# Derivative in place, two gradients transposed by DMA, and a packed score block in a four-layer transformer's forward and backward pass

## The chip, the cores and the metric

The kernel runs on one core of one Trainium2 chip. The metric is the device time of the whole program in microseconds; the median of 7 runs stands for a kernel.

## The reference

Four residual layers on x of 2048 tokens by 640, in bfloat16, with 32 heads of 20. Layers 0 and 2 (kind A) are linear attention with the features phi; layers 1 and 3 (kind B) are attention in a causal window of 256. All four have a layernorm in front and a projection behind; layers of the same kind share their weights. The outputs are x after four layers, and the gradients of x and of the four weights for a given gradient of the output.

```python
def _A_ref(x, wqkv, wo):                       # H = 32, Dh = 20
    q, k, v = ...                              # x @ wqkv, split in heads
    phi = lambda t: jnp.where(t > 0, t + 1, jnp.exp(t)) + 1e-6
    pq, pk = phi(q), phi(k)
    kv = jnp.einsum("bhsd,bhse->bhde", pk, v)
    z = jnp.einsum("bhsd->bhd", pk)
    num = jnp.einsum("bhqd,bhde->bhqe", pq, kv)
    den = jnp.einsum("bhqd,bhd->bhq", pq, z)[..., None] + 1e-6
    return ... (num / den) ... @ wo

def _B_ref(x, wqkv, wo):                       # W = 256
    scores = jnp.einsum("bhqd,bhkd->bhqk", q, k) * (Dh ** -0.5)
    mask = (idx[:, None] - idx[None, :] >= 0) & (idx[:, None] - idx[None, :] < W)
    p = _softmax(jnp.where(mask[None, None], scores, -1e9), axis=-1)
    return ... jnp.einsum("bhqk,bhkd->bhqd", p, v) ... @ wo

x = x + _A_ref(_layernorm(x), A_wqkv, A_wo);  x = x + _B_ref(_layernorm(x), B_wqkv, B_wo)
x = x + _A_ref(_layernorm(x), A_wqkv, A_wo);  x = x + _B_ref(_layernorm(x), B_wqkv, B_wo)
# outputs: x, and jax.vjp of all this at grad_out: A_x, A_wqkv, A_wo, B_wqkv, B_wo
```

The derivative of phi, where only the stored feature p = phi(t) is at hand, is min(p − 1e-6, 1).

## The kernel before

**Tiles and order.** The 2048 tokens are 16 tiles of 128. The order of the instructions of TensorE (PE), VectorE (DVE), ScalarE (ACT) and GpSimd (POOL) is the program's own: each stage is a plan, a list of pairs of a slot and a function, and a loop runs the functions slot by slot. The slots of the parts stand in tables, `PLACES`. All DMAs are issued on one queue, SyncE's (SP), in the order that a scheduler gives them. Two helpers record most of TensorE's instructions, so many rows of the profile have their lines: L138 is a matmul, L162 and the two copies at L165 and L167 are `flip`, a transpose on TensorE through the identity and its copy out of PSUM. L108 is the DMA.

**Stages.** The forward of layer 0 runs up to some 115 us. The score steps of layer 1 follow up to 400, those of layer 3 from 427 to 686; beside the steps run layernorms, projections and the rest of layer 2's linear attention as filling (`plan_front`; table `f3` has the slots beside layer 3's steps). From 690 to 1165 is the backward of layer 3's attention, from 1165 to 1285 that of layer 2's linear attention, from 1295 to 1740 that of layer 1's. From 1804 to 2031 the linear backward of layer 0 runs with the weight-gradient matmuls (`wg`, accumulated over tokens from `lhs` and `rhs` that DMAs bring from DRAM) as filling: after each slot, `fill(0.8)` gives 8 of them. What is left of the weight gradients runs alone to the end at 2251.

**Score steps.** A step is one token tile t with one group of 4 heads; 8 steps make a tile, 128 steps a layer. The keys of a tile of queries are 3 blocks of 128 tokens (from the third tile on): the far block, whose lower triangle is kept, the middle one, which is whole, and the diagonal one, whose upper triangle is kept. The scores lie with the keys on the partitions. `f_scores` (L370) does 12 matmuls of 32 rows (the padded head) by 128 keys by 128 queries, four heads in four row groups, into `sT`, a PSUM tile of four banks with one buffer; the exponential at L385 reads 4 x 384 columns of it into `eT`. `f_masks` (L388) sets the masked triangles to zero on POOL (L391 the diagonal block, L395 the far one). Two steps later `b_pv` (L213) multiplies the blocks of `eT` with v into `ops`, and `ob` (L231) divides by the sums.

**Linear backward.** `plan_linear` (L927) has the parts of one tile, table `l2`; a tile starts every 8 slots. `load` brings `ldn`, `lv`, `lpqk` (the features of q and k, [128, 2 x 640] a tile), `lhn` and `lg` for two tiles. `turn` transposes three of them. `part` (L949) makes 320 columns of the gradients of q, k or v by matmuls into PSUM; for q and k, `fd` (L969) first works out the derivative of phi for these columns, and L971 multiplies:

```python
nc.vector.scalar_tensor_tensor(out=f, in0=src(...)[:, c * CW:(c + 1) * CW], scalar=-EPS,
                               in1=self.one.to_broadcast([P, CW]), op0=ALU.add, op1=ALU.min)
nc.vector.tensor_tensor(out=dst, in0=ps[:, 0:CW], in1=f, op=ALU.mult)
```

The result `dqa` [128, 1920] holds dq, dk and dv. `dh` (L991) needs it transposed, in `dqT`: the q part by a DMA transpose (`turn_q`; layer 0's first four tiles, and none of layer 2's, by TensorE, `by_pe`), the k and v parts by `turn_kv`, 5 transposes on TensorE (L983) and a copy each, on DVE (L986) for k and on ACT (L988) for v. `dh` multiplies k, v and q in this order with the transposed weights; `ln` and `ln2` (L1004, L1014) do the layernorm's backward, with POOL's additions at L1012 and L1019. Layers 2 and 0 both use this plan.

Of the kernel before, what the change touches and what calls it, by code (L numbers as in the profile page):

```python
# [17 lines left out]
H = 32  # L18
DH = 20
HP = 32  # L20
T = 2048
TT = T // P
DT = D // P
# [17 lines left out]
PLACES = dict(  # L41
    f1=[0.1, 1.7, 2.5, 6.6, 9.6, 12, 13.2, 14.1, 14.5, 14.6, 14.5, 16.1],
    f2=[-27.5, -23.6, -21.5, -20.6, -19.5, -17.9, -16.5, -15.1, -13.5, -7.8, -6.9, -5.5, -4.7, -3.8, -2.9, 11, 12, 13, 14, 17.6, 22.4, 23.3, 24, 25.1, 26.4, 27.3],
    f3=[-35.7, -30, -26.5, -25, -24, -23.8, -22.5, -18, -16.4, -14, -12.1, -7.4, -6.8, -6, -4.9, -3.5, -1.7, 11.3, 12.4, 13.4],
    bf=[2.1, 3.1, 5.2, 14.9, 17.9, 6.2, 7.8, 10, 14.6, 28.3],
    bh=[13.1, 14.5, 15.5, 17.1, 17.5, 18, 20, 21.2, 25.7, 28.3, 30, 36, 19.1, 20.1, 21.8, 22.5, 23.3, 24.6, 25.2, 27.5, 30.5, 31.7, 33, 35, 41.5, 43, 2.2, 8.3, 9.5, 12, 18.9, 34.5],
    l2=[-10.4, -1.3, 0.6, 1.2, 1.9, 3.2, 4.6, 6.2, 7, 7.5, 5, 8, 8.3, 10.2, 11.8, 14, 14.4, 15.4, 16, 16.2, 18.7],
    n1=[9.7, 0.5, 3.3, 3.6, 5.3, 9, 3, 4.7, 5.4, 5.6, 24],
    xx=[1, 1, 0, 0, 0, 0, 1, 1, 0, 0, 0, 0, 0, 1, 0, 0, 1, 0, 0, 0, 0, 0, 0, 1, 0, 0, 1, 0, 0, 0, 1, 0],
    bd=[0, 0, 1, 0, 0, 0, 1, 0, 0, 0, 0, 0, 0, 1, 1, 0, 0, 1, 1, 0, 1, 0, 1, 0, 1, 0, 1, 1, 0, 1, 1, 0])  # L50
# [2 lines left out]
class Kern:  # L53
    def __init__(self, ctx, tc, x0, A_w, A_wo, B_w, B_wo, grad, outs):
        self.ctx, self.tc = ctx, tc
        self.nc = nc = tc.nc
        self.W = dict(A=A_w, B=B_w)
        self.Wo = dict(A=A_wo, B=B_wo)
        self.grad = grad
        self.out_x4, self.out_gx, dWA, dWoA, dWB, dWoB = outs  # L60
        self.dW = dict(A=dWA, B=dWB)
        self.dWo = dict(A=dWoA, B=dWoB)
        self.serial = 0

# [24 lines left out]
        nc.gpsimd.affine_select(out=self.bm, in_=self.bm, compare_op=ALU.is_ge, fill=0.0, base=0,  # L89
                                pattern=[[-DH, HB], [0, HA]], channel_multiplier=1)  # L90
        nc.gpsimd.affine_select(out=self.bm, in_=self.bm, compare_op=ALU.is_ge, fill=0.0, base=DH - 1,
                                pattern=[[DH, HB], [0, HA]], channel_multiplier=-1)
        self.mhalf = const.tile([P, 1], F32, name="mhalf")
        nc.gpsimd.memset(self.mhalf, -0.5)
        self.rs = [const.tile([P, TT], F32, name=f"rs{l}") for l in range(4)]
        self.r = [const.tile([P, TT, H], F32, name=f"r{l}") for l in range(4)]
        self.mz = {l: const.tile([KB, 6, KA], BF, name=f"mz{l}") for l in (0, 2)}
        self.mzT = {l: const.tile([KA, 6, KB], BF, name=f"mzT{l}") for l in (0, 2)}
        self.one = const.tile([P, 1], BF, name="one")
        nc.gpsimd.memset(self.one, 1.0)  # L100
        self.dmz = const.tile([KB, 6, KA], BF, name="dmz")
        self.dmzT = const.tile([KA, 6, KB], BF, name="dmzT")
        self.macc = const.tile([KB, 6, KA], F32, name="macc")
# [109 lines left out]
    def b_pv(self, st, l, t, g, e, nb, rings, o):  # L213
        nc = self.nc
        q = g % 4
        if q == 0:
            st.ops = st.po.tile([P, HALF, HA], F32, name="ops")
            st.first = None
        for hh in range(4):
            for i in range(nb):  # L220
                ins = self.mm(st.ops[:, 4 * q + hh, :], e[:, hh, i * P:(i + 1) * P],
                              rings[i]["s"][:, 2, 4 * g + hh, 0:HA], st.first is None, i == nb - 1)
# [12 lines left out]


    def forward(self, st):
# [11 lines left out]
        st.sm = self.pool(keep, "fm", 4, side="right")  # L249
        st.fa = self.pool(keep, "fa", 3, side="right")  # L250
        st.xm = self.pool(keep, "xm", 5, side="right")
        st.fpe = self.pool(keep, "pe", 5, side="right")
        wo = self.pool(keep, "wo", 1, side="right")
        rings = {i: self.pool(keep if i in (0, 3, 4) else early, f"ring{i}", 1, side="right") for i in (0, 3, 4, 1, 2)}
        st.fb = self.pool(early, "fb", 3, side="right")
# [87 lines left out]
        def run(n):  # L343
            u, fs = None, slots[n]
            if B1 <= n < B1 + G * TT:
                if n == B1:
                    for f in fs:
                        f()
                    fs = []
                u = self.f_scores(st, *divmod(n - B1, G), X[1])  # L350
            elif B3 <= n < END:
                u = self.f_scores(st, *divmod(n - B3, G), X[3])
# [17 lines left out]
    def f_scores(self, st, t, g, X):  # L370
# [8 lines left out]
        for i in range(nb):  # L379
            for hh in range(4):  # L380
                r0 = HP * hh
                self.mm(s[:, hh, i * P:(i + 1) * P], rings[i]["T"][r0:r0 + HP, 1, g, :], qT[r0:r0 + HP, 0, g, :],
                        True, True, (r0, 0))
        e = st.fpe.tile([P, 4, 3 * P], BF, name="eT")
        nc.scalar.activation(e[:, :, 0:nb * P], s[:, :, 0:nb * P], ACT.Exp)  # L385
        return t, g, e, nb, rings, X[t]["ob"]

    def f_masks(self, t, g, e, nb, rings, o):  # L388
        nc = self.nc
        dg = e[:, :, (nb - 1) * P:nb * P]  # L390
        nc.gpsimd.affine_select(out=dg, in_=dg, compare_op=ALU.is_ge, fill=0.0, base=0,  # L391
                                pattern=[[0, 4], [1, P]], channel_multiplier=-1)
        if nb == 3:
            fr = e[:, :, 0:P]
            nc.gpsimd.affine_select(out=fr, in_=fr, compare_op=ALU.is_ge, fill=0.0, base=-1,  # L395
                                    pattern=[[0, 4], [-1, P]], channel_multiplier=1)

    def plan_ln(self, st, l, t, x, src, key, pool):

# [527 lines left out]
    def plan_linear(self, st, lp, l, t, X, WT, g_out):  # L927
# [21 lines left out]
        def part(nm, c):  # L949
# [15 lines left out]
            if nm == "pk":  # L965
                nc.scalar.copy(dst, ps[:, 0:CW])
            else:
                f = lp.le.tile([P, CW], BF, name="fd")
                nc.vector.scalar_tensor_tensor(out=f, in0=src("pq" if nm == "dn" else "pk")[:, c * CW:(c + 1) * CW], scalar=-EPS,  # L969
                                               in1=self.one.to_broadcast([P, CW]), op0=ALU.add, op1=ALU.min)  # L970
                nc.vector.tensor_tensor(out=dst, in0=ps[:, 0:CW], in1=f, op=ALU.mult)  # L971

        def turn_q():
            x["dT"] = st.sp.tile([P, NF, P], BF, name="dqT", bufs=3)
# [3 lines left out]
                self.dma(x["dT"][:, 0:DT, :], x["dqkv"][:, 0:D], transpose=True)  # L978

        def turn_kv(j):  # L980
            ps = st.ps.tile([P, 8, P], BF, name="flip", tag="m")
            for k in range(DT):
                nc.tensor.transpose(ps[:, k, :], x["dqkv"][:, j * D + k * P:j * D + (k + 1) * P], self.ident)  # L983
# [42 lines left out]
        fs += [lambda n=n, ci=ci: dh(n, ci) for ci in range(2) for n in range(3)] + [ln, ln2]  # L1026
# [385 lines left out]
```

The softmax here doesn't subtract the row's maximum and nothing guards it: scores larger than these inputs give would overflow.

## Time and profile before

| | us |
|---|---|
| median of 7 runs | 2252.49 |
| lowest and highest | 2242.76, 2260.34 |
| profiled execution | 2252.86 |
| its span | 2251.1 |
| TensorE busy | 2076.8 |
| DVE busy | 1454.9 |
| ACT busy | 1356.7 |
| POOL busy | 1089.6 |
| mean granted clock of TensorE | 0.978 |
| DMA moved | 449.50 MB, mean 200 GB/s |

One execution is profiled; its time is 1.76 us longer than its span, the first to the last instruction. Rows of groups give the line, the engine, the operation, out<-in, shapes and count, then busy time and mean ns of one, then idle time of the engine ahead of them with what ended it. Rows of a timeline give start and length in us, and in brackets an idle time ahead and what ended it; several matmuls in one row are a run of them, and since matmuls are pipelined, rows overlap: what one holds is read from the start of the next. Rows by stage give start:end, the span, busy time and count of each engine, TensorE's granted clock, the share of the 16 DMA engines in use, and GB/s.

### The profile page before, as it was taken

The page shows a single profiled execution, that of the slowest core. Times are in us where ns is not written, and L with a number is a line of the kernel's source. Part 1 is how long each engine was busy: PE and PEld are TensorE (multiplying, and loading weights), DVE is VectorE, ACT ScalarE, POOL GpSimd, SP SyncE. Part 2 cuts the span into 40 slices and gives each one's busy share as a digit, 9 for nine tenths or more (in the row PEclk, how much of TensorE's full clock was granted, in tenths as well). Part 3 has the DMA queues.
Part 4 walks back from the last instruction along what each step waited for, and adds up shares of the span by engine and source line. Part 5 has one row for each costly group of instructions (what it writes and reads, how often), then busy time and mean ns, then how long its engine had stood idle before and what let it go on. Part 6 is the DMA issues. An engine that isn't in the chain of part 4 may idle for free. (4 is left out here: it accounts for less than half of the span.)

```text
span 2251.1 us, 76829 instructions
## 1 busy us (share of the span) xinstructions
PE 2076.8 (92%) x32061; PEld 1691.9 (75%) x32061; DVE 1454.9 (65%) x2934; ACT 1356.7 (60%) x2109; POOL 1089.6 (48%) x1888
## 2 busy tenths in 40 slices
PE   7889998899989999998979899999988899999999
PEld 5667776577767877777757678777777788889998
DVE  6778885777744788887749858787876245550000
ACT  5467887377776888887746668788876233430000
POOL 2046665156666677777534456777765312220000
PEclk9899999999999999999999989999999999999999
DMA  7489885698879589998799733999987998857753
GB/s 258 140 237 230 225 222 150 166 220 216 206 209 239 150 182 204 209 216 180 160 288 260 200 91 104 194 206 210 203 185 158 270 300 250 255 159 199 201 143 90
DMA packets 721357, 449.50 MB, mean 200 GB/s; under 512 B 461296, under 2 KB 697840, under 8 KB 720624
## 3 DMA queue, kind: packets, MB, share of 16 engines
q1 hardware_dynamic: 721008, 444.58, 77.9%
q8 instruction: 251, 4.11, 0.8%
q14 instruction: 98, 0.80, 0.1%
HBM read 213.09 MB, written 149.82 MB: 161 GB/s over the span
## 5 line engine op out<-in xcount | busy, mean ns | idle before, releaser
L665 DVE TENSOR_TENSOR ds<-dp,e 128x768 bf16<-128x768 f32 (+2 forms) x512 | 464.2, 907 | 174.6 <-PE s L138 62.9
L662 ACT ACTIVATE e<-s 128x768 bf16<-128x768 f32 (+2 forms) x512 | 395.6, 773 | 137.2 <-PE s L138 104.2
L385 ACT ACTIVATE eT<-sT 128x1536 bf16<-128x1536 f32 (+2 forms) x256 | 350.8, 1370 | 132.1 <-PE sT L138 130.2
L138 PE MATMUL wg<-rhs,lhs 128*128 128x240 bf16 (+1 forms) x3840 | 374.1, 256 | 8.8 <-DMA lhs<-o 7.3
L138 PEld LDWEIGHTS <-lhs 128*128 128x128 bf16 x3840 | 337.0, 98 | 23.9 <-DMA lhs<-o 8.3
L674 POOL TENSOR_SCALAR_AFFINE_SELECT e<-e 128x256 bf16<-128x256 bf16 x512 | 207.1, 406 | 252.0 <-ACT e L662 247.2
L138 PEld LDWEIGHTS <-dqT 128*128 128x128 bf16 x1920 | 170.6, 98 | 64.8 <-issue 10.4
L391 POOL TENSOR_SCALAR_AFFINE_SELECT eT<-eT 128x512 bf16<-128x512 bf16 x256 | 162.3, 635 | 109.6 <-ACT eT L385 108.8
L138 PE MATMUL acc<-slabqs,ds 128*128 128x20 bf16 x2880 | 210.4, 172 | 1.4 <-ACT dq L744 0.5
L138 PE MATMUL dp<-slabvT,dT 32*128 32x384 bf16 (+2 forms) x1024 | 168.7, 322 | 45.1 <-DVE ds L665 40.2
L138 PE MATMUL acc<-ds,e 128*128 128x20 bf16 x2880 | 208.3, 172 | 0.0
L138 PEld LDWEIGHTS <-ds 128*128 128x128 bf16 x2880 | 188.1, 96 | 12.0 <-issue 3.5
L678 POOL TENSOR_SCALAR_AFFINE_SELECT e<-e 128x256 bf16<-128x256 bf16 x448 | 195.9, 437 | 0.0
L138 PEld LDWEIGHTS <-e 128*128 128x128 bf16 x2880 | 170.2, 96 | 10.9 <-issue 1.8
L1012 POOL TENSOR_TENSOR dh<-dh,lg 128x640 f32<-128x640 f32 x32 | 51.5, 1609 | 254.1 <-DVE s L1009 244.8
L685 PE MATMUL flip<-ident,ds 128*128 128x128 bf16 x1944 | 170.8, 222 | 3.3 <-DVE ds L772 1.2
L138 PE MATMUL s<-slabkT,slabqT 32*128 32x384 bf16 (+2 forms) x1024 | 168.8, 325 | 4.6 <-ACT dT L797 3.3
L1094 DVE CAST wr<-wg 128x240 bf16<-128x240 f32 (+1 forms) x72 | 27.2, 378 | 222.4 <-PE wg L138 219.4
L1092 ACT CAST wr<-wg 128x240 bf16<-128x240 f32 (+1 forms) x48 | 16.3, 339 | 254.9 <-PE wg L138 227.6
L138 PE MATMUL dense<-WB,hnT 128*128 128x320 bf16 x960 | 165.3, 304 | 3.2 <-DVE o L459 1.8
L138 PE MATMUL dense<-WTA,dqT 128*128 128x320 bf16 x960 | 160.9, 299 | 3.1 <-DMA dqT<-dqa 2.7
L138 PE MATMUL acc<-slabks,dsT 128*128 128x20 bf16 x2880 | 147.4, 172 | 11.9 <-DMA dsT<-ds 11.9
(176 smaller groups left out, 4606.4 us busy)
## 6 DMA issues: line engine op xcount, KB each, us to landing
rhs<-dqkv SPq DMA_DIRECT2D x64, 480.0 KB, 4.9
s<-s SPq DMA_DIRECT2D x32, 768.0 KB, 3.8
T<-T SPq DMA_DIRECT2D x32, 768.0 KB, 3.9
dqkv<-dq SPq DMA_DIRECT2D x16, 960.0 KB, 5.6
dqkv<-dqa SPq DMA_DIRECT2D x32, 480.0 KB, 5.1
slabkT<-T SPq DMA_DIRECT2D x56, 256.0 KB, 4.3
slabvT<-T SPq DMA_DIRECT2D x56, 256.0 KB, 3.6
slabks<-s SPq DMA_DIRECT2D x56, 256.0 KB, 3.7
```

The source lines that it names most:

```text
L138: return self.nc.tensor.matmul(out, lhsT=lhsT, rhs=rhs, start=start, stop=stop, skip_group_check=True, **kw)
L385: nc.scalar.activation(e[:, :, 0:nb * P], s[:, :, 0:nb * P], ACT.Exp)
L391: nc.gpsimd.affine_select(out=dg, in_=dg, compare_op=ALU.is_ge, fill=0.0, base=0, pattern=[[0, 4], [1, P]], channel_multiplier=-1)
L662: nc.scalar.activation(u.e[:, :, 0:u.cw], s[:, :, 0:u.cw], ACT.Exp)
L665: nc.vector.tensor_tensor(out=d.ds[:, :, 0:d.cw], in0=d.dp[:, :, 0:d.cw], in1=d.e[:, :, 0:d.cw], op=ALU.mult)
L674: nc.gpsimd.affine_select(out=dg, in_=dg, compare_op=ALU.is_ge, fill=0.0, base=0, pattern=[[0, 2], [-1, P]], channel_multiplier=1)
L678: nc.gpsimd.affine_select(out=fr, in_=fr, compare_op=ALU.is_ge, fill=0.0, base=-1, pattern=[[0, 2], [1, P]], channel_multiplier=-1)
L685: nc.tensor.transpose(ps[:, 3 * j + i, :], f.ds[:, j, i * P:(i + 1) * P], self.ident)
L1012: nc.gpsimd.tensor_tensor(out=x["dh"], in0=x["dh"], in1=L["g"][:, i, :], op=ALU.add)
L1092: nc.scalar.copy(o[:, 0:w], ps[:, 0:w])
L1094: nc.vector.tensor_copy(o[:, 0:w], ps[:, 0:w])
```

## The change

Three parts.

**Derivative in place** (layers 2 and 0). The derivative of phi is worked out in place, over `lpqk`, for 640 columns at once by one tensor_scalar each for q (slot −2.3, before the `turn` of `ldn`) and k (slot 4.4, after the `turn` that reads the features of k). The four `fd` and the constant tile `one` go; L971's multiplication reads the changed `lpqk`.

```diff
-    l2=[-10.4, -1.3, 0.6, 1.2, ..., 16, 16.2, 18.7],
+    l2=[-10.4, -1.3, 0.6, 1.2, ..., 16, 16.2, 18.7, -2.3, 4.4],
...
-                f = lp.le.tile([P, CW], BF, name="fd")
-                nc.vector.scalar_tensor_tensor(out=f, in0=src("pq" if nm == "dn" else "pk")[:, c * CW:(c + 1) * CW], scalar=-EPS,
-                                               in1=self.one.to_broadcast([P, CW]), op0=ALU.add, op1=ALU.min)
-                nc.vector.tensor_tensor(out=dst, in0=ps[:, 0:CW], in1=f, op=ALU.mult)
+                nc.vector.tensor_tensor(out=dst, in0=ps[:, 0:CW], in1=src("pq" if nm == "dn" else "pk")[:, c * CW:(c + 1) * CW], op=ALU.mult)
+
+        def slope(nm):
+            nc.vector.tensor_scalar(out=src(nm), in0=src(nm), scalar1=-EPS, scalar2=1.0, op0=ALU.add, op1=ALU.min)
```

**Layer 0's k and v gradients by DMA.** From the fifth tile of layer 0 on, `turn_kv` issues a DMA transpose in place of the five transposes on TensorE and the copy; `dh`, `ln` and `ln2` of these tiles run 5 slots later.

```diff
         def turn_kv(j):
+            if lp.by_pe and t >= 4:
+                self.dma(x["dT"][:, j * DT:(j + 1) * DT, :], x["dqkv"][:, j * D:(j + 1) * D], transpose=True)
+                if j == 2:
+                    self.dma(self.rows(self.dq[l], t), x["dqkv"])
+                return
...
+        if lp.by_pe and t >= 4:
+            a = a[:13] + [v + 5 for v in a[13:21]] + a[21:]
```

**Packed scores of layer 3.** Where a step has three blocks, the far one is split by queries. Its first 64 queries go, with all keys, into columns 256 to 319. Of its last 64 queries only keys 64 to 127 can be inside the window, and these 64 x 64 scores are put where the diagonal block is masked anyway: on partitions 64 to 127, columns 128 to 191. So a head has 320 columns, the exponential reads 4 x 320, and 16 matmuls make them: 8 of 128 x 128, 4 of 128 keys by 64 queries, 4 of 64 keys by 64 queries. On POOL a first select copies the 64 x 64 scores to columns 320 to 383 with their mask, the other two mask the diagonal block and the 64 columns of the far one. The lower half of columns 320 to 383 is set to zero once in each of the five `eT` buffers, which are now a fixed list. `b_pv` takes the blocks in the order `(i + 2) % 3`.

```diff
+        if self.halves and nb == 3:
+            for c0, i, q0, n, k0 in ((0, 1, 0, P, 0), (P, 2, 0, P, 0), (2 * P, 0, 0, HALFP, 0), (P, 0, HALFP, HALFP, HALFP)):
+                for hh in range(4):
+                    score(hh, c0, rings[i], q0, n, k0)
+            w = 5 * HALFP
...
+        nc.scalar.activation(e[:, :, 0:w], s[:, :, 0:w], ACT.Exp)
...
+        if self.halves and nb == 3:
+            keep(e[HALFP:P, :, 5 * HALFP:6 * HALFP], e[HALFP:P, :, P:P + HALFP], HALFP, False)
+            dg = e[:, :, P:2 * P]
+            keep(dg, dg, P, True)
+            fr = e[:, :, 2 * P:2 * P + HALFP]
+            keep(fr, fr, HALFP, False)
...
-    f3=[-35.7, -30, -26.5, -25, -24, -23.8, -22.5, -18, -16.4, -14, -12.1, -7.4, -6.8, -6, -4.9, -3.5, -1.7, 11.3, 12.4, 13.4],
+    f3=[-35.7, -29.4, -26.6, -25, -24, -23.8, -22.2, -18, -16.5, -15, -13.1, -7.7, -6.8, -6, -4.4, -3.4, -1.7, 11.3, 12.4, 13.4],
```

More of the change, by code (lines that the diff above doesn't have):

```diff
@@ L20 @@
 HP = 32
+HALFP = P // 2
 T = 2048
@@ L43 @@
     f2=[-27.5, -23.6, -21.5, -20.6, -19.5, -17.9, -16.5, -15.1, -13.5, -7.8, -6.9, -5.5, -4.7, -3.8, -2.9, 11, 12, 13, 14, 17.6, 22.4, 23.3, 24, 25.1, 26.4, 27.3],
-    f3=[-35.7, -30, -26.5, -25, -24, -23.8, -22.5, -18, -16.4, -14, -12.1, -7.4, -6.8, -6, -4.9, -3.5, -1.7, 11.3, 12.4, 13.4],
+    f3=[-35.7, -29.4, -26.6, -25, -24, -23.8, -22.2, -18, -16.5, -15, -13.1, -7.7, -6.8, -6, -4.4, -3.4, -1.7, 11.3, 12.4, 13.4],
     bf=[2.1, 3.1, 5.2, 14.9, 17.9, 6.2, 7.8, 10, 14.6, 28.3],
     bh=[13.1, 14.5, 15.5, 17.1, 17.5, 18, 20, 21.2, 25.7, 28.3, 30, 36, 19.1, 20.1, 21.8, 22.5, 23.3, 24.6, 25.2, 27.5, 30.5, 31.7, 33, 35, 41.5, 43, 2.2, 8.3, 9.5, 12, 18.9, 34.5],
-    l2=[-10.4, -1.3, 0.6, 1.2, 1.9, 3.2, 4.6, 6.2, 7, 7.5, 5, 8, 8.3, 10.2, 11.8, 14, 14.4, 15.4, 16, 16.2, 18.7],
+    l2=[-10.4, -1.3, 0.6, 1.2, 1.9, 3.2, 4.6, 6.2, 7, 7.5, 5, 8, 8.3, 10.2, 11.8, 14, 14.4, 15.4, 16, 16.2, 18.7, -2.3, 4.4],
     n1=[9.7, 0.5, 3.3, 3.6, 5.3, 9, 3, 4.7, 5.4, 5.6, 24],
@@ L98, in __init__ @@
         self.mzT = {l: const.tile([KA, 6, KB], BF, name=f"mzT{l}") for l in (0, 2)}
-        self.one = const.tile([P, 1], BF, name="one")
-        nc.gpsimd.memset(self.one, 1.0)
         self.dmz = const.tile([KB, 6, KA], BF, name="dmz")
@@ L220, in b_pv @@
             for i in range(nb):
-                ins = self.mm(st.ops[:, 4 * q + hh, :], e[:, hh, i * P:(i + 1) * P],
+                b = (i + 2) % 3 if self.halves and nb == 3 else i
+                ins = self.mm(st.ops[:, 4 * q + hh, :], e[:, hh, b * P:(b + 1) * P],
                               rings[i]["s"][:, 2, 4 * g + hh, 0:HA], st.first is None, i == nb - 1)
@@ L251, in forward @@
         st.xm = self.pool(keep, "xm", 5, side="right")
-        st.fpe = self.pool(keep, "pe", 5, side="right")
+        fpe = self.pool(keep, "pe", 1, side="right")
+        st.fe, self.halves = [fpe.tile([P, 4, 3 * P], BF, name=f"eT{i}") for i in range(5)], False
         wo = self.pool(keep, "wo", 1, side="right")
@@ L351, in run @@
             elif B3 <= n < END:
+                if n == B3:
+                    self.halves = True
+                    for e in st.fe:
+                        nc.gpsimd.memset(e[0:HALFP, :, 5 * HALFP:6 * HALFP], 0.0)
                 u = self.f_scores(st, *divmod(n - B3, G), X[3])
@@ L378, in f_scores, with score @@
         s = st.pS.tile([P, 4, 512], F32, name="sT")
[L379 to L385, printed above, removed]
+        e = st.fe[0]
+        st.fe.append(st.fe.pop(0))
+        def score(hh, c0, k, q0, n, k0=0):
+            r0 = HP * hh
+            self.mm(s[k0:P, hh, c0:c0 + n], k["T"][r0:r0 + HP, 1, g, k0:P], qT[r0:r0 + HP, q0:q0 + n], True, True, (r0, k0))
+        qT = qT[:, 0, g, :]
+        if self.halves and nb == 3:
[3 more added lines that the diff above has]
+            w = 5 * HALFP
+        else:
+            for i in range(nb):
+                for hh in range(4):
+                    score(hh, i * P, rings[i], 0, P)
+            w = nb * P
+        nc.scalar.activation(e[:, :, 0:w], s[:, :, 0:w], ACT.Exp)
         return t, g, e, nb, rings, X[t]["ob"]
@@ L389, in f_masks, with keep @@
         nc = self.nc
[L390 to L396, printed above, removed]
+        def keep(out, in_, w, up):
+            s = 1 if up else -1
+            nc.gpsimd.affine_select(out=out, in_=in_, compare_op=ALU.is_ge, fill=0.0, base=0 if up else -1,
+                                    pattern=[[0, 4], [s, w]], channel_multiplier=-s)
+        if self.halves and nb == 3:
[4 more added lines that the diff above has]
+            keep(fr, fr, HALFP, False)
+        else:
+            dg = e[:, :, (nb - 1) * P:nb * P]
+            keep(dg, dg, P, True)
+            if nb == 3:
+                fr = e[:, :, 0:P]
+                keep(fr, fr, P, False)
     def plan_ln(self, st, l, t, x, src, key, pool):
@@ L1025, in plan_linear @@
         fs += [turn_q, lambda: turn_kv(1), lambda: turn_kv(2)]
-        fs += [lambda n=n, ci=ci: dh(n, ci) for ci in range(2) for n in range(3)] + [ln, ln2]
+        fs += [lambda n=n, ci=ci: dh(n, ci) for ci in range(2) for n in range(3)] + [ln, ln2, lambda: slope("pq"), lambda: slope("pk")]
+        if lp.by_pe and t >= 4:
+            a = a[:13] + [v + 5 for v in a[13:21]] + a[21:]
         return ([(a[0], load)] if i == 0 else []) + list(zip(a[1:], fs))
```

## The prediction

> **What bounds the kernel now.** I read the page first, then busy time by stage for the three places where the change acts, then the timelines of the engines that are full there.
>
> ```profile
> span 2251.1 us, 76829 instructions
> ## 1 busy us (share of the span) xinstructions
> PE 2076.8 (92%) x32061; PEld 1691.9 (75%) x32061; DVE 1454.9 (65%) x2934; ACT 1356.7 (60%) x2109; POOL 1089.6 (48%) x1888
> ...
> L385 ACT ACTIVATE eT<-sT 128x1536 bf16<-128x1536 f32 (+2 forms) x256 | 350.8, 1370 | 132.1 <-PE sT L138 130.2
> ```
>
> TensorE is busy for 92%, so on average little else can matter. By stage (start:end, span, then busy time of each engine, clock, DMA share, GB/s) it differs:
>
> ```profile
> 455.88:620.36 164.48, 154.91 (x2795) 119.37 (x2793) 123.84 (x321) 128.42 (x110) 101.52 (x169) 1.00 0.85 216
> 620.36:686.31 65.95, 54.39 (x1041) 42.58 (x1044) 29.75 (x74) 47.13 (x35) 44.38 (x75) 0.95 0.78 217
> 1183.38:1272.18 88.80, 81.66 (x950) 65.47 (x949) 83.03 (x157) 59.83 (x121) 39.99 (x29) 1.00 0.90 240
> 1850.00:1930.00 80.00, 80.00 (x877) 71.34 (x876) 45.30 (x89) 32.99 (x68) 18.60 (x12) 1.00 0.94 269
> 1930.00:2030.00 100.00, 100.00 (x1068) 88.70 (x1067) 51.38 (x100) 38.15 (x80) 24.73 (x16) 1.00 0.65 181
> ```
>
> Rows 1 and 2 are layer 3's forward score steps: TensorE lacks 9.6 and 11.6 us. Row 3 is layer 2's backward: DVE (83.0 of 88.8) is fuller than TensorE (81.7). Rows 4 and 5 are layer 0's backward beside weight gradients: TensorE is full, and DMA too in row 4. The clock is full but for a little in row 2.
>
> In layer 3, TensorE's timeline shows one loop through the exponential:
>
> ```profile
> 588.74 0.45 PE L138 MATMUL ops<-s,eT 128*128 128x21 bf16 x12
> 589.43 0.29 PE L138 MATMUL sT<-T,T 32*128 32x128 bf16 x8 [0.24 <-ACT eT L385]
> 589.54 0.24 PE L138 MATMUL sT<-T 32*128 32x128 bf16 x4
> 589.71 0.85 PE L138 MATMUL dense<-WB,hnT 128*128 128x320 bf16 x5
> 590.40 0.44 PE L162 MATMUL flip<-ident,o 128*128 128x128 bf16 x5
> 590.68 0.45 PE L138 MATMUL ops<-s,eT 128*128 128x21 bf16 x12
> ```
>
> The score tile sT has one buffer: its next 12 matmuls wait until the exponential has read it. A step is 1.98 us: 0.48 from the first score matmul to the exponential's start, 1.45 of exponential (128x1536), 0.05 to restart. TensorE stands 0.19 to 0.28 of each such step. Of the 8 steps of a tile, five are like this, two are bound by TensorE itself (2.03 us) and one waits 0.25 for an `ob` copy (2.44).
>
> Layer 2's DVE runs without a gap; a tile is 7.24 us, and four `fd` rows are in it:
>
> ```profile
> 1232.31 0.48 DVE L969 SCALAR_TENSOR_TENSOR fd<-lpqk,one 128x320 bf16<-128x320 bf16 x1
> 1232.88 0.49 DVE L971 TENSOR_TENSOR dqa<-dense,fd 128x320 bf16<-128x320 f32 x1
> 1233.29 1.11 DVE L969 SCALAR_TENSOR_TENSOR fd<-lpqk,one 128x320 bf16<-128x320 bf16 x1
> 1234.50 0.49 DVE L971 TENSOR_TENSOR dqa<-dense,fd 128x320 bf16<-128x320 f32 x1
> 1234.91 1.31 DVE L969 SCALAR_TENSOR_TENSOR fd<-lpqk,one 128x320 bf16<-128x320 bf16 x1
> 1236.32 0.49 DVE L971 TENSOR_TENSOR dqa<-dense,fd 128x320 bf16<-128x320 f32 x1
> ```
>
> The two long ones run beside GpSimd's additions at L1012 (1.70 us) and L1019 (1.54); the clean ones take 0.48.
>
> **Part 1, derivative in place.** Per tile four `fd` (0.48 + 1.11 + 1.31 + 0.48 = 3.38 us) become two in-place tensor_scalar of 128x640. The nearest row is L417, the same operation and shape: 0.44 clean, 0.74 at worst. DVE's work per tile falls from 6.83 (half of 13.66 in two tiles) to 6.83 − 3.38 + 0.88 = 4.3, or 6.0 if each slope met a GpSimd operation as badly as the worst `fd` (+0.84 each). Either way TensorE is next: layer 0 does the same tile in 13.14 us with 64 weight-gradient matmuls at 0.1025, so without them 13.14 − 6.56 = 6.58. DMA is close too: its share of 0.95 over 7.24 would be 1.04 over 6.6, and the most that a stretch of this trace sustains (900 to 1000 us) is 1.02, so I allow 6.75. Some 13 tiles gain 0.5 to 0.66: 6.5 to 8.6 us. The first slope runs about four slots ahead of its old reader and needs `lpqk` earlier, but that lands within 6.5 us of an issue a tile ahead; at layer 0's start it may stall DVE for 1 us. I take −7; at the low end, with DVE delayed by GpSimd, −3. In layer 0 this part costs and brings nothing: DVE is busy 45 of 80 us there.
>
> On this the Trainium skill has a rule ("SBUF — State Buffer", Who interferes with whom): DVE in a two-port mode, or with two SBUF inputs, and GpSimd hold their shared pair for a whole instruction and the loser blocks. The 1.11 and 1.31 agree. By the rule a slope could lose a whole L1012, DVE would need up to 4.3 + 2 x 1.7 = 7.7 us by an estimate from it, and the part would bring nothing.
>
> **Part 2, layer 0's k and v gradients by DMA.** For 12 tiles, 10 transposes leave TensorE:
>
> ```profile
> 1954.46 0.72 PE L983 MATMUL flip<-ident,dqa 128*128 128x128 bf16 x10
> 1955.02 0.51 PE L162 MATMUL flip<-ident,lv 128*126 128x128 bf16 x6
> ```
>
> They hold it for 1955.02 − 1954.46 = 0.56 us: 12 x 0.56 = 6.7 us, all on the path, since TensorE has no gap from here. The two copies per tile that go (DVE 0.49, ACT 0.69) were covered. Added are 24 DMA transposes on SP, each like `dqT<-dqa` now: 1.23 us of issue, 2.6 to 6.8 us to landing. SP issues some 3.7 to 5 us of work per 13 us tile, so 2.5 more fits; the loads and stores queued behind them start up to 2.5 us later. First use of k is now at slot 15.2, 7 slots of about 1.57 us after the issue, 11 us. One transpose is 640 packets of 256 B at 38 ns, 1.5 us of all 16 engines, so the share rises by 3.0/12.6 = 0.24: to 0.9 in row 5, and to 1.18 in row 4, over what 16 engines hold. Row 4 must spill about 80 x 0.16 = 13 us of DMA work into row 5, which has room; it is a delay for prefetches and only a cost if `dqT`, `lpqk` or weight-gradient loads come late. A cost is already visible at the next block's loads:
>
> ```profile
> 2074.49 11.72 PE L138 MATMUL wg<-rhs,lhs 128*128 128x160 bf16 x167 [1.81 <-DMA lhs<-o]
> ```
>
> The built order puts one more of these loads (640 KB, 2.4 us at 269 GB/s) into this last block. From −6.7 I deduct 2.4 and another 2.3 for waits in row 4: −2. The bounds are −6.7 and, with 3 us lost per tile, +32.
>
> **Part 3, packed scores.** In 112 steps the exponential reads 1280 instead of 1536 columns. Rows: 1536 take 1.450, 1024 take 1.024, so 0.832 ns a column: −0.213 us. But 16 score matmuls replace 12, and the last four are of a new shape (32x64 weights). Rounds of four start 0.06 apart (0.08 for a step with 8, 0.14 with 12), and after the last one 0.14 passes before `dense`, so a change of tile shape costs about 0.08. The extra round is thus 0.03 (half-size, no drain) to 0.11 (one more switch), up to 0.2 if loading the weights is slower in that shape. Call it d; it delays the exponential in bound steps, and adds to TensorE's work in every step. With d = 0 the five ACT steps go to 1.77, though not lower than what TensorE holds; the step at 2.44 loses part of its wait; the 2.03 steps stay. Walking through the eight steps: 15.66 us instead of 16.48; with d = 0.06, 16.14; with d = 0.12, 16.6. Ten tiles, and in the last 32 steps, where TensorE waits 0.28 to 0.56, some 22 steps that gain 0.21 − d:
> - d = 0: 10 x 0.82 + 22 x 0.21 = 12.8 us faster
> - d = 0.06: 3.4 + 3.3 = 6.7 faster
> - d = 0.12: −1.2 + 2.0, about nothing
> - d = 0.2: some 10 slower.
>
> I take d = 0.06, between an extra plain round and one with a switch: −7. GpSimd's masks go from two selects of 128x512 (0.63 each) to a half, a full and a 128x256 (0.41): 1.27 to about 1.45 us a step; at 101.5 busy of 164.5 and with two steps of lag before the products with v, that is covered; if it weren't, a step could not be under its total of about 1.5, which is still below 1.77. Five memsets run once.
>
> Here a rule speaks against the change: "TensorEngine Tiling (Array Packing)", Key Properties, says that a change of tiling mode drains TensorE, and its restrictions that column tiling disables the fast weight load. The 0.14 against 0.06 fits the first; no row here shows the second. By both rules d would be near 0.2 by an estimate, and this part a loss.
>
> **Sum.** 2252.86 − 7 − 7 − 2 = about 2236.9 us, say 2237. The profiled execution took 2252.86 (span 2251.1, 1.76 around it), 0.4 above the median of the seven runs, so the sum needs no correction.
>
> **Rivals.**
> - *The packing costs TensorE what it saves ACT* (d of 0.12 to 0.2). For it: TensorE already fills 94% of row 1. Against: five steps of eight stand still for ACT now. Layer 3 gives 0 to +10, the total is 2244 to 2254. Chance 0.16.
> - *Layer 0's DMA queue saturates* (slower). Its place is 1850 to 1930, where 0.94 becomes 1.18: if each of 12 tiles waits w for its k and v, the time is 2252.86 − 7 − 7 − 6.7 + 2.4 + 12w. It decides above w = 2.1 us (over 2259.6); 3 us gives 2271. For it: landings now reach 6.8 us at the same load. Against: 11 us of slack, and a share of only 0.65 after 1930. Chance 0.13.
> - *All of it works* (d near 0, no late transfer): 2252.86 − 12.8 − 8.6 − 6.7, 2225, down to 2215. Chance 0.11.
> - That the change doesn't do what it says is excluded by the instruction order of the built program: 120 transposes and 128 `fd` fewer, 64 slopes, 448 score matmuls and 24 DMA transposes more.
>
> **How the numbers follow.** My forecast holds 0.60, its own range 2226 to 2247. Left out of 2222 to 2256 are the lower half of the third rival and most of the second. What a measurement can tell from no change is 0.3%, 6.8 us: faster is below 2246, slower above 2259.6. Faster is 0.57 of the forecast, 0.04 of the first rival and the 0.11 of the third, 0.72; slower the 0.13 of the second; within, 0.03 and 0.12, 0.15.
>
> **What would show it.** Right: an exponential 128x1280 near 1.24 us, starting 0.54 after the first score matmul; a layer 3 tile of 16.1; no `fd`, slopes near 0.44 and DVE with gaps in layer 2, TensorE without, a tile of 6.6 to 6.8; 13.14 falling to 12.6 in layer 0 with no waits of `dense` for `dqT`. Wrong: exponentials starting later than 0.6, slopes over 1 us, a DMA wait on TensorE in every layer 0 tile, or a wait above 4 us where it is 1.81.

## The result

| | before | after |
|---|---|---|
| median, us | 2251.67 (47 runs) | 2240.79 (19 runs) |
| lowest and highest, us | 2241.6, 2260.34 | 2234.57, 2244.69 |
| profiled execution, us (span) | 2252.86 (2251.1) | 2239.54 (2237.8) |

The ratio is 0.9954, 95% interval 0.9943 to 0.9965: faster by 8 to 13 us. The prediction said 2237 with a range of 2222 to 2256. The number came out. One of the two largest terms of its sum, 7 us for the packing, did not come: the stages show that part as a small loss.

### The profile page after: what moved, and what is told of

The parts are those of the page before. It is cut to its first block, busy times and chain, and to the rows that moved or that the text cites. A ratio compares the mean times of both kernels' runs of the same rounds, so it can differ in the third digit from the quotient of the medians.

```text
span 2237.8 us, 77745 instructions
## 1 busy us (share of the span) xinstructions
PE 2085.6 (93%) x32389; PEld 1699.6 (76%) x32389; DVE 1390.0 (62%) x2858; ACT 1328.4 (59%) x2097; POOL 1111.1 (50%) x2004
## 5 line engine op out<-in xcount | busy, mean ns | idle before, releaser
L404 ACT ACTIVATE eT<-sT 128x1280 bf16<-128x1280 f32 (+3 forms) x256 | 327.0, 1277 | 154.1 <-PE sT L137 144.6
L413 POOL TENSOR_SCALAR_AFFINE_SELECT eT<-eT 128x512 bf16<-128x512 bf16 (+2 forms) x592 | 318.9, 559 | 89.7 <-ACT eT L404 56.0
L1132 DVE CAST wr<-wg 128x240 bf16<-128x240 f32 (+1 forms) x72 | 27.3, 379 | 241.5 <-PE wg L137 236.3
L1130 ACT CAST wr<-wg 128x240 bf16<-128x240 f32 (+1 forms) x48 | 16.2, 337 | 251.6 <-PE wg L137 238.5
L1048 POOL TENSOR_TENSOR dh<-dh,lg 128x640 f32<-128x640 f32 x32 | 46.0, 1437 | 237.2 <-DVE s L1045 229.0
```

Of the source, the lines that this page charges most:

```text
L404: nc.scalar.activation(e[:, :, 0:w], s[:, :, 0:w], ACT.Exp)
L413: nc.gpsimd.affine_select(out=out, in_=in_, compare_op=ALU.is_ge, fill=0.0, base=0 if up else -1, pattern=[[0, 4], [s, w]], channel_multip ...
L1048: nc.gpsimd.tensor_tensor(out=x["dh"], in0=x["dh"], in1=L["g"][:, i, :], op=ALU.add)
L1132: nc.vector.tensor_copy(o[:, 0:w], ps[:, 0:w])
```

## The profile after

The page of the changed kernel, its span, busy times and the row of the exponential (L404 now):

```profile
span 2237.8 us, 77745 instructions
## 1 busy us (share of the span) xinstructions
PE 2085.6 (93%) x32389; PEld 1699.6 (76%) x32389; DVE 1390.0 (62%) x2858; ACT 1328.4 (59%) x2097; POOL 1111.1 (50%) x2004
...
L404 ACT ACTIVATE eT<-sT 128x1280 bf16<-128x1280 f32 (+3 forms) x256 | 327.0, 1277 | 154.1 <-PE sT L137 144.6
```

TensorE is busy for 8.8 us more than before, though 120 transposes left it: something was added to it. The same stretches by engine (span, busy time and count of each, clock, DMA share, GB/s):

```profile
455.88:620.36 164.48, 163.07 (x3066) 124.50 (x3055) 119.52 (x317) 112.30 (x109) 118.71 (x246) 1.00 0.83 212
620.36:686.31 65.95, 58.72 (x1166) 46.26 (x1163) 31.60 (x76) 40.80 (x35) 48.91 (x101) 0.95 0.83 221
1183.38:1272.18 88.80, 88.50 (x1058) 72.97 (x1056) 74.19 (x147) 64.83 (x133) 38.07 (x30) 1.00 0.97 270
1850.00:1930.00 80.00, 80.00 (x862) 71.31 (x860) 27.23 (x69) 30.97 (x63) 18.17 (x12) 1.00 1.00 248
1930.00:2030.00 100.00, 100.00 (x1014) 88.55 (x1013) 27.44 (x74) 32.13 (x69) 24.18 (x16) 1.00 0.89 224
```

In layer 3 (rows 1 and 2) TensorE's idle time fell from 9.6 to 1.4 and from 11.6 to 7.2 us, but no time was won by it. In layer 2 (row 3) it is now TensorE that is full (88.5 of 88.8) and DVE that has room, with DMA at 270 GB/s instead of 240. In layer 0 (rows 4 and 5) the DMA share rose to 1.00 and 0.89, with TensorE still without a gap.

One score step of layer 3 on TensorE, the answer to the timeline shown of before:

```profile
557.47 0.24 PE L137 MATMUL sT<-T,T 32*128 32x128 bf16 x4
557.52 0.24 PE L137 MATMUL sT<-T 32*128 32x128 bf16 x4
557.58 0.36 PE L137 MATMUL sT<-T,T 32*128 32x64 bf16 x8
557.88 0.85 PE L137 MATMUL dense<-WB,hnT 128*128 128x320 bf16 x5
```

and its exponential on ACT:

```profile
558.08 1.24 ACT L404 ACTIVATE eT<-sT 128x1280 bf16<-128x1280 f32 x1 [0.66 <-PE sT L137]
```

Before, the exponential of the step shown from 589.43 stood here:

```profile
589.91 1.45 ACT L385 ACTIVATE eT<-sT 128x1536 bf16<-128x1536 f32 x1 [0.53 <-PE sT L138]
```

The exponential takes 1.24 us as predicted, but starts 558.08 − 557.47 = 0.61 us after the first score matmul (before: 589.91 − 589.43 = 0.48), and `dense` follows at 557.88 − 557.47 = 0.41 (before: 589.71 − 589.43 = 0.28). So the scores hold TensorE 0.13 us longer in such a step; the medians over the 112 steps are 0.41 and 0.28.

DVE in layer 2:

```profile
1230.42 0.62 DVE L1002 TENSOR_SCALAR lpqk<-lpqk 128x640 bf16<-128x640 bf16 x1
1231.14 0.49 DVE L998 TENSOR_TENSOR dqa<-dense,lpqk 128x320 bf16<-128x320 f32 x1
1231.55 1.57 DVE L1002 TENSOR_SCALAR lpqk<-lpqk 128x640 bf16<-128x640 bf16 x1
1233.04 0.48 DVE L998 TENSOR_TENSOR dqa<-dense,lpqk 128x320 bf16<-128x320 f32 x1
```

Two slopes of 0.62 and 1.57 stand for four `fd` of 3.38. Gaps follow further on; the median tile takes 6.59 us instead of 7.24.

## Experiments

**How the stages are read.** Each run left a profile, and the same stretches were read in all of them, in us, from the start of one instruction to that of another: *scores*, 80 steps of layer 3 (exponentials 144 to 224 of 256: ten tiles); *layer 2*, from its first multiplication `dqa` to its last; *layer 0*, from its first `dqa` to the end of the last busy instruction; and *layer 1*, the attention backward from the first `ds` to the last, which no kernel here changes. Ratios are to the kernel before on the same chip, with 95% intervals. Medians of different chips don't compare: the kernel before took 2253.85 us beside the first four runs, 2250.40 beside the next four and 2249.62 beside the last four.

| kernel | scores | layer 2 | layer 0 | layer 1 | median | ratio |
|---|---|---|---|---|---|---|
| before | 164.5 | 114.0 | 430.2 | 434.3 | 2251.67 | |
| changed | 166.9 | 102.8 | 427.3 | 427.0 | 2240.79 | 0.9954 (0.9943 to 0.9965) |
| only_slope | 164.6 | 106.2 | 431.1 | 429.0 | 2243.18 | 0.9943 (0.9924 to 0.9963) |
| only_dma | 164.5 | 114.9 | 429.9 | 431.4 | 2250.25 | 0.9977 (0.9963 to 0.9991) |
| only_pack | 166.9 | 113.7 | 430.4 | 423.7 | 2254.64 | 1.0000 (0.9988 to 1.0013) |
| slope_dma | 164.5 | 105.3 | 429.9 | 427.3 | 2241.27 | 0.9936 (0.9919 to 0.9953) |
| no_shape | 160.8 | 104.7 | 429.3 | 428.5 | 2234.99 | 0.9931 (0.9907 to 0.9955) |
| all_32x64 | 163.1 | 103.3 | 427.3 | 429.0 | 2238.81 | 0.9949 (0.9934 to 0.9965) |
| early_loads | 164.5 | 103.7 | 422.2 | 427.9 | 2228.81 | 0.9909 (0.9888 to 0.9929) |
| no_shift | 164.5 | 102.7 | 432.0 | 431.9 | 2243.33 | 0.9968 (0.9953 to 0.9983) |
| packed64_early | 163.2 | 104.6 | 421.5 | 429.6 | 2230.80 | 0.9918 (0.9902 to 0.9934) |
| packed64_old_slots | 163.4 | 103.1 | 421.9 | 427.9 | 2224.07 | 0.9893 (0.9876 to 0.9910) |
| early_again | 164.5 | 105.3 | 423.2 | 429.5 | 2231.12 | 0.9914 (0.9898 to 0.9931) |
| before_early | 164.5 | 114.2 | 428.3 | 429.7 | 2248.71 | 0.9992 (0.9979 to 1.0005) |

The column of layer 1 is the measure of chance: the same program takes 423.7 to 434.3 us there. So a few us between two profiled executions say nothing by themselves, while the scores of the ten tiles repeat within 0.3 us wherever the program of that stretch is the same.

**Each part alone.** Theory S takes the stages of the changed kernel's profile at their word; theory P is the prediction's terms; theory D asks whether the drifts in the attention backwards belong to the change.

`only_slope`: the in-place derivative in the kernel before.

```diff
+            nc.vector.tensor_scalar(out=src(nm), in0=src(nm), scalar1=-EPS, scalar2=1.0, op0=ALU.add, op1=ALU.min)
             # layer 0's transposes and layer 3's scores and slots as before
```

> Only the derivative in place; scores and layer 0's transposes as before. Theory S (the changed kernel's profile read by stages): layer 2's tile falls from 7.24 to 6.58 us and its 16 tiles bring 9 to 11 us, time 2241 to 2243, ratio 0.995. Theory P (the prediction's term): 7 us, ratio 0.997. Theory D (the drifts of +3.5 and -7 us that the two profiles show in the attention backwards are carried by the change and not by chance): layer 1's backward is 7 us shorter here too, 16 to 18 us in all, ratio 0.9925.

0.9943, 8 to 17 us faster: the interval lies above P's 7, and holds S and the near end of D. The stage gives 114.0 − 106.2 = 7.8 here. All ten kernels with the part have 102.7 to 106.2, the four without 113.7 to 114.9: 10 us between the means.

`only_dma`: the DMA transposes of layer 0 in the kernel before.

```diff
+            if lp.by_pe and t >= 4:
+                self.dma(x["dT"][:, j * DT:(j + 1) * DT, :], x["dqkv"][:, j * D:(j + 1) * D], transpose=True)
             # four fd and layer 3's scores and slots as before
```

> Only layer 0's k and v gradients by DMA transposes. Theory S: layer 0's backward gains 7 us up to its last tile and 4 us are given back in the loads of the last block, 3 us in all, ratio 0.9987. Theory P: 2 us, ratio 0.999. If nothing were given back: 6.7 us, 0.997. Tiles in the middle of layer 0 of 12.6 us instead of 13.1; a wait of weight-gradient matmuls for lhs of 2.7 us instead of 1.8.

0.9977, 2 to 8 us faster. The tiles in the middle of layer 0 take 12.61 us (median) instead of 13.14, as forecast. But the stage gains only 0.3 in this profile and 2.9 in the changed kernel's, of 6.7 that leave TensorE. Here 1.6 us of it went to longer waits for `rhs<-g` at the layer's start, and at its end TensorE waits 3.6 us for `lhs<-o`, not 2.7. Between S and no give-back the times don't decide; the waits do, below.

`only_pack`: the packed scores and the shifted slots in the kernel before.

```diff
+            for c0, i, q0, n, k0 in ((0, 1, 0, P, 0), (P, 2, 0, P, 0), (2 * P, 0, 0, HALFP, 0), (P, 0, HALFP, HALFP, HALFP)):
             # four fd and layer 0's transposes as before
```

> Only the packed scores, with the shifted slots. Theory S: 0.13 us more of score matmuls a step against 0.21 us less of exponential; a tile of eight steps takes 16.66 instead of 16.48 us, layer 3 ends 3 us later, ratio 1.0014. Theory P: 7 us faster, 0.997. Theory D: the end of layer 3's backward is 8 us later, ratio 1.0035.

1.0000, within 2.8 us of nothing: P's 0.997 and D's 1.0035 are out, and S's 1.0014 lies just beyond the interval's end. The ten tiles are 2.4 us longer, 16.69 each, as in the changed kernel; the last 32 steps up to the first `ds` take 74.6 against 73.3, so the gain that was expected there isn't there either. D falls in layer 1 too: it took 423.7 us here, 429.0 and 431.4 in the other two, in no order that follows the parts.

The 1.3 us lie behind the steps. The time from the last exponential's start to the first `ds` is 8.7 to 9.0 us in all six kernels with the packing and 7.3 to 7.5 in the eight without. In the last 32 steps and behind them the products with v wait 2.7 to 3.8 us for GpSimd's masks on `eT` with the packing, 0.5 to 1.5 without. No run changes the masks alone, so this cause is read from the waits and not tested.

`slope_dma`: the whole change without the packing.

```diff
-                if n == B3:
-                    self.halves = True
...                # and f3 as before
```

> The whole change without the packing (score blocks and slots of layer 3 as before). Theory S: the two parts add, 12 to 14 us faster, ratio 0.994, and 3 us faster than the changed kernel. Theory P (packing worth 7 us): 9 us, ratio 0.996, slower than the changed kernel by 2 us or more. Theory D: 16 to 20 us, 0.992.

0.9936 beside 0.9954 of the whole change: leaving out one of the three parts loses nothing. It may win 4 us, but the intervals overlap; the stage, 164.5 against 166.9, says 2.4 for ten tiles of the fourteen.

**What the packing pays for.** `no_shape` keeps all 16 matmuls but gives the last four the shape of the rest. It leaves out the scores of the far block's last 64 queries.

```diff
-            ... (2 * P, 0, 0, HALFP, 0), (P, 0, HALFP, HALFP, HALFP)):
+            ... (2 * P, 0, 0, HALFP, 0), (5 * HALFP, 0, HALFP, HALFP, 0)):
```

> The changed kernel, but the fourth round of score matmuls has the shape of the others: 128 keys by 64 queries into the unused columns 320 to 383, so the far block's last 64 queries get no scores of their own (they are left out of the result); the number of matmuls, exponential, masks and slots stay. Theory S (the switch between tile shapes costs 0.09 us, and a plain round 0.04): the exponential starts 0.52 to 0.55 us after the first score matmul instead of 0.61, a tile of eight steps takes 15.9 to 16.2 us instead of 16.66, the kernel is 5 to 9 us faster than the changed one, ratio to before 0.992. Theory R (the extra round costs 0.13 whatever its shape): 0.61, 16.66, ratio 0.9952.

A step of it on TensorE, and its exponential on ACT:

```profile
526.93 0.24 PE L137 MATMUL sT<-T,T 32*128 32x128 bf16 x4
526.99 0.24 PE L137 MATMUL sT<-T 32*128 32x128 bf16 x4
527.04 0.24 PE L137 MATMUL sT<-T,T 32*128 32x64 bf16 x8
527.22 0.85 PE L137 MATMUL dense<-WoB,obT 128*128 128x320 bf16 x5
```

```profile
527.42 1.24 ACT L404 ACTIVATE eT<-sT 128x1280 bf16<-128x1280 f32 x1 [0.54 <-PE sT L137]
```

The exponential starts after 0.49 us instead of 0.61, and `dense` after 0.29 instead of 0.41, nearly the 0.48 and 0.28 of the kernel before with its 12 matmuls. The extra round costs 0.01; the other 0.12 comes with the last four, whose weights are 32x64 in the changed kernel. A tile takes 16.08 instead of 16.69. Theory S, with the switch dearer and the round cheaper than it said; R's 0.61 and 16.66 are out, though its 0.9952 still lies in the ratio's interval. The run changes one thing besides the shape: in the changed kernel the last four overwrite columns that the second round has just written, here they write columns of their own. The next run keeps the overwriting.

`all_32x64`: every score matmul of a packed step as 32x64 tiles.

```diff
-                for hh in range(4):
-                    score(hh, c0, rings[i], q0, n, k0)
+                for hh in range(4):
+                    for kk in ks:                  # ks: (0, 1), for the last round (1,)
+                        score(hh, c0, rings[i], q0, n, kk * HALFP, (kk + 1) * HALFP)
```

> The changed kernel, but every score matmul of a packed step is a 32x64 tile, two for a block of 128 keys (28 matmuls instead of 16), so that no shape changes within a step. Theory S: only the switch is gone and the two halves run side by side; the exponential starts at 0.50 to 0.54 us, a tile takes 15.9 to 16.2, ratio 0.992. Rival (weights of 32x64 tiles load slower, or 28 matmuls take their starts one after the other): it starts at 0.65 us or later, a tile takes 17 us or more, ratio 0.998 or above.

```profile
528.63 0.26 PE L137 MATMUL sT<-T,T 32*64 32x128 bf16 x8
528.69 0.26 PE L137 MATMUL sT<-T 32*64 32x128 bf16 x8
528.74 0.27 PE L137 MATMUL sT<-T,T 32*64 32x64 bf16 x12
528.94 0.85 PE L137 MATMUL dense<-WoB,obT 128*128 128x320 bf16 x5
```

Neither as S nor as its rival had it. TensorE pays 528.94 − 528.63 = 0.31 us for 28 matmuls, hardly more than for 12: the halves do run side by side. With the overwriting kept and the change of shape gone, 0.10 of TensorE's 0.13 are gone, so the change of shape is what they were paid for. But the exponential starts after 0.58 (at 529.21), not 0.52; the last score matmul begins after 0.19, as against 0.13 with 12, and where the rest comes from stays open. A tile takes 16.31: 0.38 less than with the mixed shapes, 0.14 less than without packing. So in the ten tiles the packing's sign is turned. Over all 112 steps up to the first `ds` it isn't shown: 238.2 us here, 237.5 and 237.3 in the two later kernels with this packing, 237.4 to 238.5 in the eight without, 242.4 and 241.5 with the mixed shapes. What the tiles win, the longer end gives back.

**What layer 0's DMAs give back.** TensorE at the end of `slope_dma`, as weight gradients go over to a new `lhs`:

```profile
2017.83 37.01 PE L137 MATMUL wg<-rhs,lhs 128*128 128x240 bf16 x366
2055.89 0.45 PE L137 MATMUL wg<-rhs,lhs 128*128 128x160 bf16 x4 [1.05 <-DMA lhs<-o]
2057.73 0.45 PE L137 MATMUL wg<-rhs,lhs 128*128 128x160 bf16 x4 [1.39 <-DMA lhs<-o]
2059.47 20.72 PE L137 MATMUL wg<-rhs,lhs 128*128 128x160 bf16 x259 [1.29 <-DMA lhs<-o]
```

and the stretches around it:

```profile
2056.00:2060.00 4.00, 1.33 (x13) 0.93 (x13) 0.00 (x0) 0.00 (x0) 0.00 (x0) 0.77 0.93 280
2060.00:2064.00 4.00, 4.00 (x33) 4.00 (x31) 0.32 (x1) 0.00 (x0) 0.00 (x0) 0.50 0.52 124
...
2066.00:2070.00 4.00, 4.00 (x62) 4.00 (x59) 0.33 (x1) 0.29 (x1) 0.00 (x0) 1.00 0.12 25
```

Three waits of 3.7 us together where the kernel before has one of 1.8; and after them the granted clock is 0.50, so that 4 us do 33 matmuls instead of 62. It stays there from 2058.15 to 2064.97; TensorE is busy for 5.53 us of that, at half the clock, so some 2.8 us are lost by it. Before, no drop followed the single wait (clock 1.00 from 2072 to 2076). The six loads stand in SyncE's queue behind stores of weight gradients that wait for their values:

```profile
2044.08 0.81 SPq L107 DMA_DIRECT2D out_dram<-wr  x1
2044.94 4.93 SPq L107 DMA_DIRECT2D lhs<-o  x6
```

`early_loads` puts them into the program of `slope_dma` a block of weight gradients earlier:

```diff
+                if m == 3 and not W.tight and k + 2 < len(todo) and todo[k + 2][3] == 0:
+                    soon = [lhs(x) for x in todo[k + 2][0]]
...
-                    nxt = [lhs(L2[0]), None if W.tight else lhs(L2[1])], nxt[1]
+                    nxt = [lhs(L2[0]), None] if W.tight else soon, nxt[1]
```

> Derivative in place and layer 0's DMA transposes without the packing, and the loads lhs<-o of the last block put into the program one block of weight gradients earlier. Theory T (what part 2 gives back at the end is TensorE's wait for these loads, 3.7 us there, and the clock of 0.5 that follows it for some 4 us): no wait for lhs<-o after 2030 us, no granted clock below 1.0 there, 4 to 5 us faster than the kernel with the two parts alone, ratio 0.9915. Rival (the loads are bound by the DMA engines and not by their place in SyncE's queue): the wait moves to other loads, rhs<-g or rhs<-dqkv, ratio 0.9936 as without the edit.

SyncE's queue, then stretches of the same end:

```profile
2024.67 8.46 SPq L107 DMA_DIRECT2D lhs<-o  x8
```

```profile
2040.00:2060.00 20.00, 20.00 (x260) 19.70 (x259) 1.79 (x5) 0.94 (x3) 0.00 (x0) 1.00 0.84 211
2060.00:2080.00 20.00, 20.00 (x292) 20.00 (x290) 1.63 (x6) 1.17 (x4) 0.00 (x0) 1.00 0.87 219
```

No wait, no drop of the clock, and layer 0 at 422.2 instead of 429.9 us. The loads land no faster, about one every 2 us in both kernels, and the engines are full under them (a share of 1.07 from 2045 to 2058 in `slope_dma`); but the first of the block is issued some 14 us earlier in the early kernel, counted from layer 0's first `dqa`. So it was the place in the queue and not what the DMA engines can carry.

`before_early`: the same edit in the kernel before.

> The kernel before with the early loads alone. Theory T: its wait for lhs<-o is 1.8 us and no drop of the clock follows it, so 2 us, ratio 0.999. Rival (the early loads are worth 5 us or more whatever the rest does): 0.9975 or less.

0.9992 and 428.3 against 430.2: as T said, 2 us, though the ratio's interval holds nothing too; the rival is out. In the kernels with part 2 the edit is worth 5 to 6 us by the ratios and 6 by the means of layer 0's stage. Two of these were there to win before; the other 3 to 4 are what part 2 had given back. The stage says the same from the other side: with the early loads layer 0 takes 421.5 to 423.2 us with part 2 and 428.3 without, 5 to 7 us, which is about the 6.7 that left TensorE.

`no_shift`: `dh` of `slope_dma` at its old slots.

```diff
-            a = a[:13] + [v + 5 for v in a[13:21]] + a[21:]
+            a = a[:13] + [v + 0 for v in a[13:21]] + a[21:]
```

> The two parts without the packing, and layer 0's dh, ln and ln2 at their old slots: 2.2 slots, some 3.5 us, from the k transpose's issue to its first use instead of 11. Theory T: transposes land 4.4 us after their issue or later, so that dense waits for dqT in nearly every one of the 12 tiles, 1 to 3 us each, 12 to 30 us in all; ratio 0.999 to 1.007. Rival (the slack was not needed): no such waits, and the end is 2 to 4 us earlier for the five slots saved, ratio 0.992.

Neither: the ratio, 0.9968 (0.9953 to 0.9983), lies between the two. TensorE's waits in layer 0:

```profile
PE dense L137 <- DMA dqT<-dqa: 6.3, 5, 2.9
```

Five waits of 6.3 us in all, not one in nearly every one of the twelve tiles; with the shift there is none. Layer 0 takes 432.0 us against 429.9, and `slope_dma` had a ratio of 0.9936. The loss is smaller than the waits because the loads at the end were late by less: TensorE waits 1.6 us for `lhs<-o` there instead of 3.7, and no drop of the clock follows. The slack was needed, though 3.5 us cover more of the transposes than the theory said.

**Together.**

`packed64_early` has the edits of `all_32x64` and `early_loads`:

> The changed kernel with both edits: every score matmul of a packed step as a 32x64 tile, and the loads lhs<-o one block earlier. Theory S (packing in one shape is worth 0.13 us a tile of eight steps, 1 to 3 us in all, and adds to the early loads): 1 to 3 us faster than the kernel without packing beside it, ratio to before 0.989 to 0.990. Rival (packing in any form is worth nothing): the same as without it, 0.991.

0.9918 (0.9902 to 0.9934): the rival's 0.991 lies in the interval, S's 0.989 to 0.990 just outside.

`packed64_old_slots` takes the slots back besides:

```diff
-    f3=[-35.7, -29.4, -26.6, ...],
+    f3=[-35.7, -30, -26.5, ...],          # the whole table as before the change
```

> As the run before, with layer 3's table of slots as it was before the change. Theory: the shifted slots only move filling work from one step to another, so the sum over a tile, which TensorE binds in most steps, differs by less than 0.2 us, 3 us in all. Rival (the new slots are what lets TensorE fill its gaps): a tile is 0.3 us or more longer, the kernel 4 us or more slower.

The slots of layer 3 make no difference where they act: 163.4 and 163.2. The rival is out. The median is 6.7 us lower than that of the run before, more than the theory's 3; the intervals overlap, and nothing in layer 3 shows a reason.

`early_again` is `early_loads` once more:

> Derivative in place, layer 0's DMA transposes and early loads, no packing, again, beside the two runs with packing. Expected as measured: ratio 0.991.

It repeats: 0.9914 after 0.9909.

The kernel with everything and the old slots, 2224.07 us, 0.9893 (0.9876 to 0.9910), beats both the kernel before and the changed one (0.9954, from 0.9943). Whether packing in one shape beats none stays open in the totals (0.9893 and 0.9918 against 0.9914, all overlapping); in the ten tiles it is 1.2 us, and up to the first `ds` the means differ by 0.5, within the spread.

## Why the prediction was right in sum

**Layer 2** (−7, measured −10). The mechanism held: DVE was the bound and TensorE, at the 6.58 us read from layer 0, came next. Two steps were too careful: the tile was raised to 6.75 for DMA, whose share at 6.58 is 0.97 and not the 1.04 scaled up from 0.95; and 13 tiles were counted of 16. In 13 of the 16 tiles a slope meets GpSimd's second addition, L1019 before and L1055 now (mostly 1.57 us, of which 1.39 lie beside it, against 0.32 alone); with the other slope's 0.62 that makes 2.2 us, where 0.88 was the clean price and 2.56 the worst that was allowed. Slopes over 1 us were a sign of being wrong, but it cost nothing, since DVE kept room: 74.2 of 88.8. The 6.5 us in which `lpqk` was said to land are a median (4.6 to 9.8); slopes waited for it twice, 1.0 us in all. The Trainium skill's rule on the shared pair ("SBUF — State Buffer", Who interferes with whom) agrees with these rows; the price that I had worked out from it, a tile of 7.7 on DVE, did not come.

**Layer 0** (−2; the stage is 0.3 to 2.9 us shorter than before in the five kernels that have the part with its shift and without the early loads). The 6.7 held: tiles of 12.61 us instead of 13.14, 6.4 in twelve. Of the two deductions one was in the right place: the load at the end, priced at 2.4, was 1 to 2 us of longer wait plus 2 to 3 us of halved clock, which the sum had no term for. The 2.3 us for waits beside a full DMA did not come: at a share of 1.00 the transposes landed within 8.4 us, and 11 were there.

**Layer 3** (−7, measured none; the ten tiles +2.4). This is the step that failed, and its sign came: an exponential that starts later than 0.6. The delay d was taken as 0.06 between a plain round (0.03) and one with a switch (0.11), and it is 0.13, of which the switch is 0.12. The price of a switch, 0.08, was read from the gap between the last score matmul and `dense`; that gap was the nearest row, but not of the same kind. With d = 0.12 the prediction's own walk through a tile gives 16.6; 16.69 was measured. At small d the walk was too generous as well: `no_shape`, with d near 0.01, takes 16.08, where it gave 15.66 for 0. TensorE is busy for 15.80 us of these 16.08, so it had little left to give. On a straight line between the two kernels d = 0.06 would give 16.33, by an estimate, 0.12 less than the 16.45 of before, where the sum had 0.34 less than 16.48 (its own eight steps add up to 16.40). The third thing that failed is the end of the layer: the masks came to 1.47 us a step, as priced (1.45), but there, by TensorE's waits, they were not covered: the last 32 steps with what follows up to the first `ds` lost 1.3 to 2.2 us, where a gain of 2.0 was forecast for d = 0.12. So it was the first rival that came for this part, and the other stages hid it in the sum. The Trainium skill ("TensorEngine Tiling (Array Packing)", Key Properties) had said that changing the mode drains the engine: it spoke for the end of the range that came true. The page's restriction on weight loads under column tiling (Restrictions) shows in no run here as slower starts: 28 such matmuls begin within 0.19 us.

The rest of the 13.3 us between the two profiles lies in stages that the change doesn't touch: layer 1's backward was 7.2 us shorter, layer 3's 3.5 longer. With layer 2's 11.2, layer 0's 2.9, and 4.6 lost in layer 3's scores and behind them, that makes 13.2. Since the same program spreads over 10.6 us in layer 1, it is taken as chance. That the measured time lies within 4 us of 2237 is thus partly luck: of the 7 us that did not come, 3 came from layer 2 beyond its forecast, and the rest of what made up for them is these drifts.

## What to carry to other kernels

Taking work from one engine pays only up to what the next one holds in that very stage: 0.21 us off the exponential was worth nothing because TensorE was 94% full there and got 0.13 more. When a small matmul of another tile shape joins a group, price the change of shape and not the columns; giving the whole group the small shape can be cheaper (16.31 us a tile against 16.69 here). And after each saving look at the end of its stage: a load that was just in time is now late, and moving its issue in the program was worth 5 to 6 us here, about as much as the second part could bring at all.

## What was not expected of the hardware

- A change from 32x128 to 32x64 weights between matmuls of one group cost 0.12 us here; 28 matmuls of 32x64 held TensorE for 0.31 us where 12 of 32x128 held it for 0.28.
- Three waits of 3.7 us in all, with 4 matmuls between each, brought a granted clock of 0.50 for 6.8 us; in the changed kernel two waits of 2.7 us in all brought it for 3.4 us; one wait of 1.8 us did not. The Trainium skill ("TensorE: Matmul & The Clock Gate", Part 1) tells of a free-running window of 3.4 us that has to be idle or busy. The lengths agree with one and two such windows; but no wait in those two kernels was longer than 1.39 us, so no such window was idle throughout. In the 3.4 us before the drop TensorE was busy for 0.97 us in the one and 0.74 in the other; what share is enough no run here shows.
- The in-place tensor_scalar of 128x640 takes 0.32 us, not the 0.44 of the row with two per-partition scalars.
